# A decode step (cached attention plus GeGLU gate): the last wo rows cut by partitions, x in two loads, wo's first quarter ahead of w_down, 14 drains on SP

## The chip, the core and the metric

The kernel runs on one core of a Trainium2 chip, as one launch. The metric is device time in microseconds (us); of several executions the median is taken. Lower is better.

## The reference, cut to what matters

One token for each of 8 sequences goes through a layernorm, then through two branches that both read the normed row: attention over the last 1024 positions of a cache (32 query heads, 8 key/value heads of 128), projected by wo, and a gated feed-forward net. The second branch gates the first.

```python
xn = layernorm(x)                                   # x: 8 x 512, bf16
q  = xn @ wq                                        # wq: 512 x 4096
p  = softmax(q @ k[last 1024].T * 128**-0.5)        # k, v: 8 x 8 x 4096 x 128; 16 MB each are read
s  = (p @ v[last 1024]) @ wo                        # wo: 4096 x 512
f  = (gelu(xn @ w_gate) * (xn @ w_up)) @ w_down     # 512 x 1792 twice, 1792 x 512
out = x + s * silu(f)
```

## The kernel before, in words

Everything is in one function, and its order is written out by hand: each engine runs its instructions in the order of the source.

**Loads.** Nearly all loads are issued from SP's queue, in this order: wo's first quarter (`wo_first`, L106), wq (L109), then K and V of the eight sequences, each as two transfers of 1 MB (`load_cache`, L84), then w_gate and w_up (L426), w_down (L429), and wo's other three quarters (L439). The last quarter of wo comes in three pieces along its 8 rows per partition: rows 0 to 4, 5 to 6, and row 7 alone (1 KB in each of 128 partitions). x (8 rows of 1 KB) comes in four loads of two rows from ACT's queue (L79). The tile framework gives every DMA one of eight completion semaphores in turn. A DMA waits on its issuing queue until the one that had its semaphore before has landed, so at most eight are under way. K and V go through a ring of eight buffers; two of these use wq's memory once q is computed.

**Attention.** For each sequence: DVE turns K (`turn_k`, L248), PE makes the scores (L309), DVE and ACT do the softmax, PE makes the values (L354), and `gather` (L374) and `regroup` (L376 to L398) put the outputs of four sequences at a time into `oT`, the stationary operand of the wo product.

**The end.** After the last `regroup`, PE runs in this order: z and u (xn by w_gate and w_up, L453), then f (the hidden row by w_down, L482, 28 matmuls), then s (`oT` by wo, L501, 64 matmuls: quarters u = 0 to 3, rows j = 0 to 7, two halves each). Between u and f stands a chain on ACT and DVE, the gelu (L463 to L473), that ends in the transpose `hT` (L476). The last product is gated and added to x (L509, L511), and two DMAs write the output (L514). The quarter u = 0 reads `wo_first`, which was loaded at the very start.

```python
for u in range(NU):                      # L498
    for j in range(8):
        for t in range(NT):
            nc.tensor.matmul(s_ps[32*t : 32*t + 32, :], oT[:, j, u, :],
                             wo[u][:, j, t*DT : (t+1)*DT], ...)
```

Of the kernel before, what the change touches and what calls it, by code (L numbers as in the profile page):

```python
# [11 lines left out]
FP32 = mybir.dt.float32  # L12
# [8 lines left out]
def kernel(  # L21
# [13 lines left out]
    nc = tc.nc  # L35
# [9 lines left out]
    P = nc.NUM_PARTITIONS  # L45
# [7 lines left out]
    NT = 2  # L53
    DT = D // NT
# [12 lines left out]
    def slot(name):  # L67
        i = taken[0] % N_SLOTS
        taken[0] += 1
        if i >= 2:  # L70
            return ring.tile([P, 2 * ROW], BF16, name=name, tag="slot")
        if not late:
            late.append(ctx.enter_context(tc.tile_pool(name="late", bufs=2)))
        return late[0].tile([P, 2 * ROW], BF16, name=name, tag="slot")


    x_sb = keep.tile([B, D], BF16, name="x_sb")
    for r, z in ((0, 2), (2, 4), (4, 6), (6, 8)):
        nc.scalar.dma_start(out=x_sb[r:z], in_=A_x.flatten_outer_dims()[r:z])  # L79

    def load_cache(cache, b, name):
        t = slot(name).rearrange("p (g x) -> p g x", g=NG)
        for g in range(NG):
            nc.sync.dma_start(  # L84
                out=t[:, g],
                in_=cache[b, g * HG : (g + 1) * HG, win0:Sk, :].rearrange(
                    "n (p c) d -> p n (c d)", c=C
                ),
            )
        return t  # L90
# [3 lines left out]
    def load_k(b):  # L94
        k_sb[b] = load_cache(A_k_cache, b, "k_sb")

    def load_v(b):
        v_sb[b] = load_cache(A_v_cache, b, "v_sb")

    NU = Hq // 8  # L100
    wo_src = [
        A_wo[u * 1024 : (u + 1) * 1024, :].rearrange("(p j) d -> p j d", j=8)
        for u in range(NU)
    ]
# [6 lines left out]
    load_k(0)  # L111
    load_k(1)
    load_v(0)


    ident = consts.tile([P, P], BF16, name="ident")
# [2 lines left out]
        out=ident,  # L119
        in_=ident,  # L120
# [13 lines left out]
        out=xpad,  # L134
        in_=xpad,
# [17 lines left out]
        out=xhat,  # L153
# [8 lines left out]
    with tc.tile_pool(name="ps_x", bufs=1, space=PSUM) as ps_x:  # L162
# [7 lines left out]
        for t in range(NT):  # L170
# [4 lines left out]
                start=True,  # L175
                stop=True,
# [12 lines left out]
        out=hv,  # L189
        in_=hv,  # L190
# [7 lines left out]
        out=neg_st,  # L198
        in_=neg_st,
# [8 lines left out]
        out=neg_mv,  # L208
        in_=neg_mv,
# [11 lines left out]
    for g in range(NG):  # L221
        nc.vector.tensor_reduce(
            out=sel[:, g, g * qd : (g + 1) * qd],
            in_=ident.rearrange("p (t g h) -> p g h t", t=4, g=NG)[:, g],
# [5 lines left out]
        out=own, in_=ident.rearrange("p (i e) -> p e i", e=8), axis=AX.X, op=ALU.add  # L230
    )
    pick = consts.tile([P, 4 * NU], BF16, name="pick")
    with nc.allow_low_precision(reason="sums of zeros and a single one"):
        nc.vector.tensor_reduce(
            out=pick, in_=ident.rearrange("p (a e) -> p a e", e=8), axis=AX.X, op=ALU.add
        )
    oT = keep.tile([P, 8, NU, 32], BF16, name="oT")
# [18 lines left out]
    with tc.tile_pool(name="ps_q", bufs=1, space=PSUM) as ps_q:  # L256
        q_ps = [ps_q.tile([P, 512], FP32, name=f"q_ps{i}") for i in range(8)]
        for k in range(NK):
            for i in range(8):
# [4 lines left out]
                    start=(k == 0),  # L264
                    stop=(k == NK - 1),
                )
        for half in range(2):
            for i in range(4 * half, 4 * half + 4):
                e = nc.vector.tensor_copy if i % 4 == 3 else nc.scalar.copy
# [7 lines left out]
    for j in range(4):  # L277
        sl = slice(32 * j, 32 * j + 32)
        for m in range(2):
            for g in range(NG):  # L280
                e = nc.scalar.copy if (4 * j + 2 * m + g) % 3 == 2 else nc.vector.tensor_copy
# [148 lines left out]
    wo = [wo_first]  # L430
    for u in range(1, NU):
        if u % 2 == 1:
            pair = slot("wo_sb").rearrange("p (v j d) -> p v j d", v=2, d=D)
        t = pair[:, (u - 1) % 2]
        pieces = [(0, 8)]
        if u == NU - 1:
            pieces = [(0, 5), (5, 7), (7, 8)]
        for a, z in pieces:
            nc.sync.dma_start(out=t[:, a:z, :], in_=wo_src[u][:, a:z, :])  # L439
        wo.append(t)  # L440

    gather(B - 1)
# [3 lines left out]
    ps_f = ctx.enter_context(tc.tile_pool(name="ps_f", bufs=1, space=PSUM))  # L446
    ffn = ctx.enter_context(tc.tile_pool(name="ffn", bufs=1))
    zu = []
    for n, ws in (("z_ps", wgu[0]), ("u_ps", wgu[1])):
        ps = ps_f.tile([P, FT], FP32, name=n)  # L450
        for k in range(NK):
            for t in range(4):
# [4 lines left out]
                    start=(k == 0),  # L457
                    stop=(k == NK - 1),
# [6 lines left out]
        out=z2, in0=z2, scalar1=0.044715, scalar2=1.0, op0=ALU.mult, op1=ALU.add  # L465
# [10 lines left out]
    nc.vector.transpose(  # L476
        out=hT.rearrange("p j b -> p (j b)"), in_=h_bf.rearrange("p (y j) -> p j y", j=NJ)
    )
    f_ps = ps_f.tile([32 * NT, DT], FP32, name="f_ps")
    for j in range(NJ):  # L480
        for t in range(NT):
# [4 lines left out]
                start=(j == 0),  # L486
                stop=(j == NJ - 1),
# [4 lines left out]
        out=g_sb, in0=g_sb, scalar1=0.5, scalar2=0.5, op0=ALU.mult, op1=ALU.add  # L492
# [1 line left out]
    nc.vector.tensor_tensor(out=g_sb, in0=g_sb, in1=f_ps, op=ALU.mult)  # L494


    s_ps = ps_f.tile([32 * NT, DT], FP32, name="s_ps")
    for u in range(NU):  # L498
        for j in range(8):
            for t in range(NT):  # L500
                nc.tensor.matmul(  # L501
                    s_ps[32 * t : 32 * t + 32, :],
                    oT[:, j, u, :],
                    wo[u][:, j, t * DT : (t + 1) * DT],
                    start=(u == 0 and j == 0),
                    stop=(u == NU - 1 and j == 7),
                )
    y = ffn.tile([32 * NT, DT], BF16, name="y")
    nc.vector.tensor_tensor(out=y, in0=s_ps, in1=g_sb, op=ALU.mult)  # L509
    out_sb = ffn.tile([32 * NT, DT], BF16, name="out_sb")  # L510
# [2 lines left out]
    for t, e in ((0, nc.sync), (1, nc.scalar)):  # L513
        e.dma_start(  # L514
            out=out_f[:, t * DT : (t + 1) * DT], in_=out_sb[32 * t : 32 * t + B, :]
# [31 lines left out]
```

## Time and profile before

| | |
|---|---|
| median of 3 runs | 120.83 us (120.79 to 120.89) |
| the profiled execution's own time | 120.78 us |
| its span, first to last instruction | 118.9 us |
| busy: PE / DVE / ACT / POOL | 62% / 64% / 28% / 3% of the span |
| DMA | 47.57 MB, mean 400 GB/s; SP's queue took 95.0% of 16 engines' span |
| K and V loads, issue to landing | 19.6 us for 1 MB |

The profile's page cuts the span into 40 equal slices of 2.97 us. A digit is a busy share in tenths; PEclk is the clock that the throttle granted to TensorE. The chain of waits is followed back from the last instruction, at each step to what released it. Idle time of an engine that is not on that chain costs nothing by itself. A table by windows gives busy time of each engine, the granted clock and the mean busy share of the 16 DMA engines for stretches of the span.

### The profile page before, as it was taken

The page shows a single profiled execution, that of the slowest core. Times are in us where ns is not written, and L with a number is a line of the kernel's source. Part 1 is how long each engine was busy: PE and PEld are TensorE (multiplying, and loading weights), DVE is VectorE, ACT ScalarE, POOL GpSimd, SP SyncE. Part 2 cuts the span into 40 slices and gives each one's busy share as a digit, 9 for nine tenths or more (in the row PEclk, how much of TensorE's full clock was granted, in tenths as well). Part 3 has the DMA queues.
Part 4 walks back from the last instruction along what each step waited for, and adds up shares of the span by engine and source line. Part 5 has one row for each costly group of instructions (what it writes and reads, how often), then busy time and mean ns, then how long its engine had stood idle before and what let it go on. Part 6 is the DMA issues. An engine that isn't in the chain of part 4 may idle for free.

```text
span 118.9 us, 1553 instructions
## 1 busy us (share of the span) xinstructions
PE 74.1 (62%) x610; PEld 35.2 (30%) x610; DVE 75.8 (64%) x101; ACT 33.1 (28%) x83; POOL 3.2 (3%) x10
## 2 busy tenths in 40 slices
PE   0000279941599596969964867598299263854990
PEld 0000123410233253435432324134035131413780
DVE  1002779389998999999956995980994224165102
ACT  2100600096202518171531341071070811110100
POOL 2000430000000000000000000000000000000000
PEclk9999999999679999999999999679859955555599
DMA  3999899999999999999999999999999999999940
GB/s 59 472 453 431 353 433 427 419 438 427 427 424 427 430 424 422 427 419 435 427 408 435 433 422 430 433 422 424 424 430 419 459 415 444 405 426 430 412 153 3
DMA packets 6103, 47.57 MB, mean 400 GB/s; under 512 B 696, under 2 KB 848, under 8 KB 1104
## 3 DMA queue, kind: packets, MB, share of 16 engines
q1 hardware_dynamic: 6064, 47.45, 95.0%
q8 instruction: 5, 0.08, 0.2%
q10 hardware_dynamic: 32, 0.01, 0.0%
q14 instruction: 2, 0.02, 0.0%
HBM read 47.46 MB, written 0.01 MB: 399 GB/s over the span
## 4 chain that ended last, share of the span: by engine, by line
DMA 60%; PE 24%; DVE 9%; ACT 3%; issue 1%; SPq 0%; DVEq 0%
DMA k_sb<-in_A_k_cache_dram 49%; DMA wq_sb<-in_A_wq_dram 12%; PE q_ps L260 8%; PE S_ps L309 5%; PE s_ps L501 3%; PE f_ps L482 3%; DVE kT L248 2%; PE O_ps L354 2%; PE z_ps L453 1%; PE o_ps L374 1%; ACT P_sb L332 1%; DVE o_x L381 1%; DVE mx L319 1%; DVE hT L476 1%; ACT nb L329 1%
## 5 line engine op out<-in xcount | busy, mean ns | idle before, releaser
L309 PE MATMUL S_ps<-kT,qbd 128*128 128x512 bf16 x128 | 35.0, 421 | 16.2 <-DVE kT L248 12.8
L248 DVE STREAM_TRANSPOSE kT<-k_sb 128x2048 int32<-128x2048 int32 x16 | 36.5, 2289 | 5.2 <-DMA k_sb<-in_A_k_cache_dram 5.2
L309 PEld LDWEIGHTS <-qbd 128*128 128x128 bf16 x128 | 13.0, 103 | 35.4 <-issue 20.3
L329 ACT ACTIVATE nb<-m 32x1 f32<-32x1 f32 x32 | 6.4, 201 | 23.5 <-DVE m L326 23.2
L332 ACT ACTIVATE P_sb<-S_ps,nb 128x1024 bf16<-128x1024 f32 x8 | 11.1, 1391 | 0.3
L354 PE MATMUL O_ps<-v_sb,pT 128*32 128x256 bf16 x256 | 9.3, 292 | 2.7 <-DVE pT L344 2.7
L260 PE MATMUL q_ps<-wq_sb,xnR 128*128 128x512 bf16 x32 | 9.5, 469 | 2.4 <-DMA wq_sb<-in_A_wq_dram 2.4
L319 DVE TENSOR_REDUCE mx<-S_ps 128x1 f32<-128x1024 f32 x8 | 9.6, 1195 | 1.8 <-PE S_ps L309 1.8
L366 ACT COPY O_sb<-O_ps 128x256 f32<-128x256 f32 x8 | 3.0, 374 | 21.6 <-PE O_ps L354 21.6
L354 PEld LDWEIGHTS <-pT 128*32 128x32 bf16 x256 | 6.5, 102 | 6.3 <-issue 3.0
L166 PE MATMUL xnT_ps<-ident,xhat 8*128 8x8 bf16 x4 | 0.3, 174 | 12.6 <-DVE xhat L152 12.6
L344 DVE STREAM_TRANSPOSE pT<-P_sb 128x512 int32<-128x512 int32 x8 | 5.7, 712 | 3.4 <-ACT P_sb L332 3.0
L145 DVE BATCH_NORM_STATS2 stats<-x_sb 8x6 f32<-8x512 bf16 x1 | 0.7, 681 | 9.4 <-DMA x_sb<-in_A_x_dram 9.4
L374 PE MATMUL o_ps<-O_sb,sel 128*32 128x129 f32 x32 | 5.5, 297 | 1.0 <-ACT O_sb L366 1.0
L260 PEld LDWEIGHTS <-xnR 128*128 128x128 bf16 x32 | 3.6, 115 | 8.0 <-issue 5.9
L298 PE MATMUL S_ps<-neg_mv,neg_st 128*128 128x512 bf16 x16 | 4.8, 382 | 1.9 <-DVE q_both L270 1.9
L270 ACT CAST q_both<-q_ps 128x512 bf16<-128x512 f32 x6 | 3.0, 611 | 10.0 <-PE q_ps L260 10.0
L482 PE MATMUL f_ps<-wd_sb,hT 128*32 128x256 bf16 x28 | 3.2, 419 | 3.1 <-DVE hT L476 3.1
L374 PEld LDWEIGHTS o_ps<-O_sb,sel 128*32 128x32 f32 x32 | 3.1, 116 | 4.9 <-issue 3.1
L251 DVE MEMSET qbd<- 128x4096 uint32 x1 | 3.5, 3472 | 0.8 <-issue 0.8
L166 PEld LDWEIGHTS <-xhat 8*128 8x128 bf16 x4 | 0.2, 114 | 12.6 <-DVE xhat L152 12.6
L501 PEld LDWEIGHTS <-oT 128*32 128x32 bf16 x64 | 3.6, 107 | 0.7
(64 smaller groups left out, 51.1 us busy)
## 6 DMA issues: line engine op xcount, KB each, us to landing
k_sb<-in_A_k_cache_dram SPq DMA_DIRECT2D x16, 1024.0 KB, 19.6
v_sb<-in_A_v_cache_dram SPq DMA_DIRECT2D x16, 1024.0 KB, 19.6
wq_sb<-in_A_wq_dram SPq DMA_DIRECT2D x1, 4096.0 KB, 14.2
wo_sb<-in_A_wo_dram SPq DMA_DIRECT2D x2, 1024.0 KB, 25.0
wgu_sb<-in_B_w_gate_dram SPq DMA_DIRECT2D x1, 1792.0 KB
wgu_sb<-in_B_w_up_dram SPq DMA_DIRECT2D x1, 1792.0 KB
wd_sb<-in_B_w_down_dram SPq DMA_DIRECT2D x1, 1792.0 KB
wo_first<-in_A_wo_dram SPq DMA_DIRECT2D x1, 1024.0 KB, 4.9
```

The costliest lines, as they stand in the source:

```text
L248: nc.vector.transpose(out=t.bitcast(I32), in_=k_sb[b][:, g].bitcast(I32))
L260: nc.tensor.matmul(q_ps[i], xnR[:, k, :, :].rearrange("p j b -> p (j b)"), wq_sb[k][:, i * 512 : (i + 1) * 512], start=(k == 0), stop=(k = ...
L298: nc.tensor.matmul(S[b][:, half, :], neg_st.rearrange("p j h -> p (j h)"), neg_mv.rearrange("p a n -> p (a n)"), start=True, stop=False,)
L309: nc.tensor.matmul(S[b][:, half, :], qbd[:, m, b, w, g, :], kv[:, half * 16 : (half + 1) * 16, m, :, w], start=False, stop=(g == NG - 1 an ...
L319: nc.vector.tensor_reduce(out=mx, in_=S[b].rearrange("p a c -> p (a c)"), axis=AX.X, op=ALU.max)
L329: nc.scalar.mul(nb[32 * j : 32 * j + 32, :], m1, -inv)
L332: nc.scalar.activation(out=P_sb[b].rearrange("p c i w -> p c w i"), in_=S[b].rearrange("p a (c w i) -> p (a c) w i", w=2, i=32), func=ACT.Exp,
L344: nc.vector.transpose(out=pT[b].rearrange("p c h w -> p (c h w)").bitcast(I32), in_=P_sb[b].rearrange("p c i w -> p (c i w)").bitcast(I32),)
L354: nc.tensor.matmul(O_ps[b][32 * t : 32 * t + 32, :, :], pT[b][:, c // 2, :, c % 2], vv[:, c, :, :], start=(c < 4), stop=(c >= C - 4),)
L374: nc.tensor.matmul(o, sel[:, g, :], O_sb[b][:, g, :], start=(g == 0), stop=(g == NG - 1))
L482: nc.tensor.matmul(f_ps[32 * t : 32 * t + 32, :], hT[:, j, :], wd[:, j, t * DT : (t + 1) * DT], start=(j == 0), stop=(j == NJ - 1),)
L501: nc.tensor.matmul(s_ps[32 * t : 32 * t + 32, :], oT[:, j, u, :], wo[u][:, j, t * DT : (t + 1) * DT], start=(u == 0 and j == 0), stop=(u = ...
```

## The change

- The last quarter's row 7 (`(7, 8)`, 1 KB in each of 128 partitions) is no longer one transfer: partitions 0 to 31, 32 to 116 and 117 to 127 are loaded by a transfer each (32, 85 and 11 partitions), from the same queue.
- x comes in two loads of four rows, not four of two.
- The s product of quarter u = 0 (16 matmuls) stands before the f product, in PE's order; quarters 1 to 3 stay behind it. The tile `s_ps` is allocated earlier.
- 14 drain instructions stand on SP's queue behind the first three K/V loads. With the two added transfers, SP's program goes from 76 to 92 instructions.

```diff
-    for r, z in ((0, 2), (2, 4), (4, 6), (6, 8)):
+    for r, z in ((0, 4), (4, 8)):
         nc.scalar.dma_start(out=x_sb[r:z], in_=A_x.flatten_outer_dims()[r:z])
...
     load_k(0)
     load_k(1)
     load_v(0)
+    for _ in range(14):
+        nc.sync.drain()
...
-        pieces = [(0, 8)]
+        pieces = [(0, 8, 0, P)]
         if u == NU - 1:
-            pieces = [(0, 5), (5, 7), (7, 8)]
-        for a, z in pieces:
-            nc.sync.dma_start(out=t[:, a:z, :], in_=wo_src[u][:, a:z, :])
+            pieces = [(0, 5, 0, P), (5, 7, 0, P), (7, 8, 0, 32), (7, 8, 32, 117), (7, 8, 117, P)]
+        for a, z, r, e in pieces:
+            nc.sync.dma_start(out=t[r:e, a:z, :], in_=wo_src[u][r:e, a:z, :])
...
+    s_ps = ps_f.tile([32 * NT, DT], FP32, name="s_ps")
+
+    def project(u):
+        for j in range(8):
+            for t in range(NT):
+                nc.tensor.matmul(
+                    s_ps[32 * t : 32 * t + 32, :],
+                    oT[:, j, u, :],
+                    wo[u][:, j, t * DT : (t + 1) * DT],
+                    start=(u == 0 and j == 0),
+                    stop=(u == NU - 1 and j == 7),
+                )
+
+    project(0)
     f_ps = ps_f.tile([32 * NT, DT], FP32, name="f_ps")
...
-    s_ps = ps_f.tile([32 * NT, DT], FP32, name="s_ps")
-    for u in range(NU):
...
+    for u in range(1, NU):
+        project(u)
```

More of the change, by code (lines that the diff above doesn't have):

```diff
@@ L494 @@
     nc.vector.tensor_tensor(out=g_sb, in0=g_sb, in1=f_ps, op=ALU.mult)
-    s_ps = ps_f.tile([32 * NT, DT], FP32, name="s_ps")
-    for u in range(NU):
[L499 to L507, printed above, removed]
+    for u in range(1, NU):
+        project(u)
     y = ffn.tile([32 * NT, DT], BF16, name="y")
```

## The prediction

> **What bounds the kernel now.** I read the page first, then the windows and the chain of waits at the end, then the waits of PE and SP. In the 40 slices (part 2 of the page):
>
> ```profile
> PEclk9999999999679999999999999679859955555599
> DMA  3999899999999999999999999999999999999940
> GB/s 59 472 453 431 353 433 427 419 438 427 427 424 427 430 424 422 427 419 435 427 408 435 433 422 430 433 422 424 424 430 419 459 415 444 405 426 430 412 153 3
> ```
>
> The DMA engines are full from the second slice to slice 38, at about 427 GB/s, and TensorE's clock is at half from about 95 us until shortly before the end. So the stream of bytes sets nearly everything, and what remains is how the last bytes and the last matmuls meet. The chain of waits over the last 11 us, in order of time (start, length, what):
>
> ```profile
> 107.65 0.99 DVE hT L476
> 108.64 0.04 issue
> 108.69 3.17 PE f_ps L482 x28
> 111.86 4.00 PE s_ps L501 x60
> 115.86 0.02 issue
> 115.88 0.43 DVE y L509
> ```
>
> By this the end is compute: f, then s without a gap. The windows (length, busy time of PE, PEld, DVE, ACT, POOL, granted clock, DMA share, GB/s) show the transfers beside it:
>
> ```profile
> 105.89:109.31 3.42, 0.62 (x8) 0.45 (x10) 2.57 (x4) 0.00 (x0) 0.00 (x0) 0.50 0.96 408
> 109.31:112.72 3.41, 3.41 (x36) 2.49 (x34) 0.31 (x2) 0.38 (x1) 0.00 (x0) 0.50 0.99 416
> 112.72:114.10 1.38, 1.38 (x28) 1.25 (x26) 0.39 (x1) 0.00 (x0) 0.00 (x0) 1.00 0.83 320
> 114.10:115.50 1.40, 1.40 (x30) 1.26 (x27) 0.00 (x0) 0.00 (x0) 0.00 (x0) 1.00 0.25 87
> ```
>
> The last row matters most: for 1.4 us only a quarter of the DMA engines still works. The trace's completion events of the last transfer (row 7 of wo's last quarter) say the same: ten of its 16 parts end at 113.93 to 114.15 us, two at 114.65 and 114.77, four at 115.34 to 115.50. The piece before it (rows 5 and 6) ends at 115.165, rows 0 to 4 at 114.566, wo's third quarter at 113.022. The last pair of matmuls starts at 115.561. So PE is on the chain, but the last bytes stand only 0.06 us behind it: two bounds that coincide.
>
> Why six engines are late can be read too. The page's DMA queues show instruction loads:
>
> ```profile
> q8 instruction: 5, 0.08, 0.2%
> q14 instruction: 2, 0.02, 0.0%
> ```
>
> By the start of their packets they come at 33.6 and 57.4 us (8 KB) and 44.5, 59.1, 84.2, 99.8 and 114.8 us (16 KB). Behind each of the first six, one more engine's completions fall back, by 0.7 to 0.9 us for 8 KB and 1.3 to 1.8 us for 16 KB, and stay behind to the end, since SP's queue is never empty. Two light and four heavy ones are the two and four above.
>
> **The change part by part.** The sum is made against the profiled execution, 120.78 us (span 118.9 us and 1.9 around it), 0.05 under the median.
>
> *Quarter 0 before f.* It takes 16 matmuls from between f and quarter 1. They start at 111.65 and quarter 1 at 113.05: 1.40 us off PE's last stretch. They go where PE waits:
>
> ```profile
> PE f_ps L482 <- DVE hT L476: 3.1, 1, 3.1
> ```
>
> u ends at 105.58 and f may start at 108.69. At the half clock a pair takes 0.209 us (f's rows), so 8 pairs take 1.67: 105.4 to 107.2. `oT` was ready at 102.17, wo_first at 5.7. Cover left: 1.4 us, so no cost. If the cover were gone, f would wait up to 1.67 us. The clock rose at 112.72, after a window that PE had filled; f and quarter 1 fill the same window. The window before it becomes about 0.5 busy, where ones of 0.72 and 0.78 raised nothing. So f stays at half clock until 111.65, then quarter 1: five pairs at 0.209 to 112.72, three at 0.108, to 113.03. Quarter 2 finds its bytes (113.022) and runs to 113.93. Then PE waits, for the first time in this stretch. From completion to the matmul it released took 0.043 us (w_up at 103.843, u at 103.886). Row 0 of quarter 3 starts at 114.61, row 5 at 115.165 + 0.043 = 115.21, row 6 at 115.32, row 7 at 115.425 or at its own landing plus 0.043, the later. With the old row 7 transfer that is 115.544: 0.017 us gained of 1.40. What is late next is the transfer.
>
> *Row 7 in three.* In this trace the engines of one transfer always take equal shares: x's 2-row load completes in two steps, the 8-row output in eight, 128 rows in 16 of 8 rows each. So 32 rows go as 2 to each of 16. 85 is 5 times 17, so equal shares mean 5 engines with 17 rows or one with 85; 11 rows mean 11 with one. The price of a row: between rows 5 to 6 and row 7 the slowest engine spent 0.336 us on 8 rows, 0.042 each. An engine outside the five carries 2 or 3 rows, not 8, and lands 0.21 to 0.25 us sooner; one of the five carries 19 or 20, 0.46 to 0.50 later. If the four heavy engines are outside, row 7 lands at 115.25 to 115.31 with a completion packet or two more (0.01 each), under the 115.38 at which row 6 gives way; the ten on time reach 114.6, a light one 115.27. The bounds are far apart: the 85 rows on all 16 engines give nothing (115.50), on one engine alone 85 x 0.042 = 3.6 us, so 117.5 from an engine on time. I take five, since one is the extreme and no transfer here is uneven. Whether the four are outside the five is the open question. I followed packets by their start times from the two engines that carried x's rows: neither met a 16 KB load before 114 us, one perhaps the 8 KB load at 57.4 (engines in the same phase can't be told apart, so this is weak). If x's two are of the five, four heavy ones miss the other three with about 0.33 if strewn at random over 14, about 0.7 if they are neighbours. I take 0.6, the likelier side.
>
> The Trainium skill ("DMA: Bandwidth & Descriptors", Why a DMA increments its semaphore by 16 and not by 1) says that a transfer uses the largest number up to 16 that divides its slowest dimension, on the lowest-numbered engines: 16, 5 and 11 here. The trace agrees for 2, 8 and 128 rows; no run here shows 85. The Trainium skill's same page (Rules for kernel authors) speaks against the change: cutting a transfer by partitions isn't worth it, and under 64 KB one pays mostly overhead. By its table's figure for 64 KB, 0.95 us (measured on loads issued from GpSimd), an estimate for three in a row would be 2.85 us, 2.5 more than now; the trace's last piece, 128 KB queued behind another, cost 0.34 us, so it disagrees, and this gets no chance of its own.
>
> *x in two loads.* Two loads less on ACT, 0.24 us each, beside nothing. SP's waits name x:
>
> ```profile
> SPq L84 <- DMA x_sb<-in_A_x_dram: 3.2, 2, 1.9
> SPq L84 <- DMA wq_sb<-in_A_wq_dram: 4.3, 1, 4.3
> ```
>
> x's later rows land behind big packets of the other queue (5.7, 8.1, 10.6 us), so two loads land by about 5.7, and the layernorm moves up 5 us. It still ends at wq, landed at 15.47. SP may issue two K/V loads sooner, into a queue that is full anyway. Zero, hidden by wq; at most the 0.1 us of a few packets either way.
>
> *14 drains.* SP's drains last 7 to 13 ns and its instructions stand 0.06 us apart, so 0.2 to 0.9 us on SP, with the next K load behind them. It finds 9 us of wq ahead of it in the queue: hidden; without that cover, 0.9. But a longer program can load one block more: ACT (97 recorded instructions) and DVE (117) each did, SP (72) did not, and it will have 88. By where 88 lies between 72 and 97, I give that 0.6. It costs one engine 0.7 us, nothing unless it is one of the four late ones (1 in 4).
>
> Sum: row 7's pair at 115.425 instead of 115.561, 0.14 less; 120.64 for the profile, 120.69 for the median. That is within 0.2% (0.24 us), about what a measurement of this kernel can tell from no change. Terms unsure by 0.05 each and the completion delays put it between 120.45 and 120.9.
>
> **The rivals.**
> - *A heavy engine is among the five* (slower). Place: row 7's 85-row transfer; price: 12 rows more on a late engine, 0.50, so 116.00 + 0.043 instead of 115.561. 121.31, with 121.2 to 121.4 around it. It decides as soon as one of the four takes part. For: five of 16 is much. Against: x's engines looked clean. Chance 0.23.
> - *SP's own load falls on a late engine*: 0.7 us behind the rest at the end, 115.30 + 0.7 + 0.043 against 115.561, so 121.3. Chance 0.6 x 0.25, less what counts above: 0.08.
> - *The longer program moves the loads to better places.* If no heavy engine is late at the end but the light ones (114.77) are, row 7's pair starts near 114.85 to 115.0, and 0.55 to 0.7 us go: 120.2. For: lateness is all that holds the end above 114.1, and 14 drains touch only program layout. Against: five loads follow TensorE's count, which does not change. Chance 0.20.
> - *The split does nothing* (85 rows on all engines): only 0.02 of the move is left, 120.81. Chance 0.04.
>
> **How the numbers follow.** Forecast 0.45: a third of it (0.15) lies beyond 0.24 us, 0.01 above. Faster 0.15 + 0.20 = 0.35; same 0.29 + 0.04 = 0.33; slower 0.01 + 0.23 + 0.08 = 0.32. The range, 120.2 to 121.4, takes in both sides and leaves out about 0.15. The forecast's own is 120.45 to 120.9.
>
> **What would show it.** 16 s matmuls between 105.4 and 107.2 us; a wait of PE for wo_sb of about 0.7 us before row 0 of quarter 3; row 7's last completion at 115.25 to 115.31; PE's last pair at 115.42; no new stretch of idle DMA before 113 us. Wrong: row 7 landing near 116.0 (the five hold a late engine); a third 8 KB load and a fifth late engine; a different count of late engines at the end; f starting later than 108.7.

## The result, and the profile after

The changed kernel takes 120.95 us (median of 21 executions, 120.77 to 121.45), against 120.79 us (120.50 to 121.16) for 21 executions of the kernel before on the same chip. The ratio is 1.0021, 95% interval 1.0013 to 1.0029. The forecast was 0.14 us less; measured is 0.16 us more by the medians, 0.25 by the ratio.

The profiled execution is one of the changed kernel's fastest: 120.80 us, span 119.1 (the median span is 119.2) and 1.7 around it (before: 118.9 and 1.9). The page's clock and DMA slices, its instruction loads and its chain:

```profile
PEclk9999999999589999999999999999769955577699
DMA  2998899999999999999999999999999999999930
q8 instruction: 5, 0.08, 0.3%
q14 instruction: 4, 0.02, 0.1%
DMA 95%; PE 1%; DVE 1%; issue 0%; SPq 0%
```

The stream is as full as before. There are two more instruction loads on q14: 8 KB at 118.47 us, and 80 bytes at the span's start. The chain that ended last is now DMA to 95%; before, its end was PE. The same chain piece by piece (start, length, what):

```profile
90.28 24.36 DMA wo_sb<-in_A_wo_dram
114.64 0.04 issue
114.68 1.29 PE s_ps L486 x16
115.98 0.02 issue
116.00 0.43 DVE y L516
```

f and 44 of the 60 s matmuls have left it: the end now hangs on wo's last quarter. The gated product `y` starts at 116.00, against 115.88 before. The timeline of the last 12 us shows how PE got there (start, length, line, operation, idle before and its releaser in brackets):

```profile
105.11 1.22 PE L486 MATMUL s_ps<-wo_first,oT 128*32 128x256 bf16 x16
...
108.40 2.77 PE L498 MATMUL f_ps<-wd_sb,hT 128*32 128x256 bf16 x28 [2.07 <-DVE hT L478]
...
110.96 1.69 PE L486 MATMUL s_ps<-wo_sb,oT 128*32 128x256 bf16 x16
...
112.82 1.05 PE L486 MATMUL s_ps<-wo_sb,oT 128*32 128x256 bf16 x16 [0.17 <-DMA wo_sb<-in_A_wo_dram]
...
114.68 1.28 PE L486 MATMUL s_ps<-wo_sb,oT 128*32 128x256 bf16 x16 [0.82 <-DMA wo_sb<-in_A_wo_dram]
```

Quarter 0 runs in the wait for `hT`, which still leaves 2.07 us of it. Quarters 2 and 3 now wait for their bytes, 0.17 and 0.82 us. Quarter 3 then takes 1.28 us, where 1.05 is a quarter without a wait at full clock: its last pair starts at 115.677, after row 7. The windows (length, busy time of PE, PEld, DVE, ACT, POOL, granted clock, DMA share, GB/s):

```profile
105.45:108.86 3.41, 1.34 (x26) 1.02 (x24) 2.61 (x4) 0.08 (x1) 0.00 (x0) 1.00 0.96 407
108.86:112.28 3.42, 3.42 (x38) 2.53 (x34) 0.56 (x2) 0.38 (x1) 0.00 (x0) 0.50 1.00 422
112.28:114.10 1.82, 1.42 (x22) 1.04 (x19) 0.14 (x1) 0.00 (x0) 0.00 (x0) 1.00 0.87 333
114.10:115.70 1.60, 1.02 (x16) 0.69 (x15) 0.00 (x0) 0.00 (x0) 0.00 (x0) 1.00 0.18 60
```

The last row is the place of the change. Before, a quarter of the DMA engines still worked for the last 1.4 us; now 0.18 of them, for 1.6 us. Row 7's bytes did end sooner: the last completion packet runs at 114.971 us, before at 115.214. But the completions come later behind their packets. In us, by the trace's DMA packets and completion events:

```
                                          before    after   forecast
wo rows 0 to 4, last completion          114.566  114.640  114.566
wo rows 5 and 6, last completion         115.165  115.272  115.165
row 7: last completion packet            115.214  114.971
row 7: last completion                   115.501  115.541  115.25 to 115.31
  of it 32 / 85 / 11 partitions             -     115.422 / 115.359 / 115.541
from that packet to that completion        0.287    0.570
last pair of s matmuls starts            115.561  115.677  115.425
output, last landing                     118.095  118.178
from that landing to the span's end        0.830    0.908
```

The last two lines count too. From the last pair to the output's landing it is 2.53 us before and 2.50 after; behind the landing SP still has its last waits to work through, and there the change loses another 0.08 us.

### The profile page after: what moved, and what is told of

Read it like the earlier page. It is cut to its first block, busy times and chain, and to the rows that moved or that the text cites. A ratio compares the mean times of both kernels' runs of the same rounds, so it can differ in the third digit from the quotient of the medians.

```text
span 119.1 us, 1559 instructions
## 1 busy us (share of the span) xinstructions
PE 71.7 (60%) x603; PEld 35.3 (30%) x610; DVE 76.0 (64%) x101; ACT 33.1 (28%) x83; POOL 3.2 (3%) x10
## 4 chain that ended last, share of the span: by engine, by line
DMA 95%; PE 1%; DVE 1%; issue 0%; SPq 0%
DMA v_sb<-in_A_v_cache_dram 71%; DMA wo_sb<-in_A_wo_dram 20%; DMA wo_first<-in_A_wo_dram 4%; PE s_ps L486 1%; DVE y L516 0%; DVE out_sb L518 0%; SPq L441 0%
## 5 line engine op out<-in xcount | busy, mean ns | idle before, releaser
L311 PE MATMUL S_ps<-kT,qbd 128*128 128x512 bf16 x128 | 33.2, 406 | 18.6 <-DVE kT L250 15.1
L486 PE MATMUL s_ps<-wo_sb,oT 128*32 128x256 bf16 x48 | 4.0, 310 | 1.0 <-DMA wo_sb<-in_A_wo_dram 1.0
L300 PE MATMUL S_ps<-neg_mv,neg_st 128*128 128x512 bf16 x9 | 3.3, 384 | 1.9 <-DVE q_both L272 1.9
L272 DVE CAST q_both<-q_ps 128x512 bf16<-128x512 f32 x2 | 1.3, 672 | 3.9 <-ACT q_both L272 3.9
```

Source lines behind the costliest of these rows:

```text
L272: e(out=q_bf[:, i * 512 : (i + 1) * 512], in_=q_ps[i])
L311: nc.tensor.matmul(S[b][:, half, :], qbd[:, m, b, w, g, :], kv[:, half * 16 : (half + 1) * 16, m, :, w], start=False, stop=(g == NG - 1 an ...
L486: nc.tensor.matmul(s_ps[32 * t : 32 * t + 32, :], oT[:, j, u, :], wo[u][:, j, t * DT : (t + 1) * DT], start=(u == 0 and j == 0), stop=(u = ...
```

## The experiments

The theories that the expectations name. **P**: transfers over part of the partitions make the engines' completions late. **W**: each further small transfer costs by itself, whatever its form. **F**: PE's last 16 KB instruction load, which moved up to 113.9 us, slows the late engines. **D**: the drains decide which engines are late. B, C, X and N are explained where they first stand; C of e7 and e8 is another theory than C of e12. The table puts all runs together, each against the kernel before on the same chip. Its last two columns are of the one profiled execution: the start of the last pair of s matmuls (of e9's second matmul), and the time from the output's last landing to the span's end.

| kernel | SP's instructions | median us | ratio to before | median span | time less span | last pair | landing to end |
|---|---|---|---|---|---|---|---|
| before (beside each) | 76 | 120.67 to 120.79 | | 118.8 to 118.9 | 1.86 to 1.89 | 115.561 | 0.830 |
| the change | 92 | 120.95 | 1.0021 [1.0013, 1.0029] | 119.2 | 1.73 | 115.677 | 0.908 |
| e1: the move alone | 76 | 120.72 | 1.0002 [0.9989, 1.0016] | 118.85 | 1.87 | 115.738, half clock | 0.823 |
| e2: the split alone | 78 | 121.22 | 1.0044 [1.0028, 1.0059] | 119.3 | 2.02 | 115.882 | 0.987 |
| e3: the change, row 7 whole | 90 | 121.16 | 1.0042 [1.0030, 1.0054] | 119.5 | 1.74 | 115.995, half clock | 1.393 |
| e4: the change, no drains | 78 | 121.37 | 1.0055 [1.0040, 1.0070] | 119.25 | 2.11 | 115.691 | 0.883 |
| e5: x in two alone | 76 | 120.85 | 1.0018 [1.0004, 1.0031] | 119.0 | 1.87 | 115.775 | 0.944 |
| e6: 16 drains alone | 92 | 120.61 | 0.9991 [0.9982, 0.9999] | 118.9 | 1.71 | 115.449 | 0.835 |
| e7: row 7 as 48, 48, 32; 14 drains | 92 | 121.64 | 1.0080 [1.0060, 1.0099] | 119.9 | 1.73 | 116.081 | 1.348 |
| e8: row 7 as 125, 3; 15 drains | 92 | 120.73 | 0.9999 [0.9988, 1.0010] | 119.0 | 1.77 | 115.463 | 0.839 |
| e9: row 7 in column halves; 15 drains | 92 | 120.84 | 1.0014 [1.0002, 1.0026] | 119.1 | 1.73 | 115.587 | 1.040 |
| e10: row 7 in partition halves; 15 drains | 92 | 121.03 | 1.0028 [1.0017, 1.0040] | 119.3 | 1.73 | 115.749 | 1.044 |
| e11: 2 drains alone | 78 | 121.00 | 1.0017 [1.0006, 1.0028] | 118.9 | 2.09 | 115.310 | 0.823 |
| e12: the move, PE kept busy, 16 drains | 92 | 120.59 | 0.9987 [0.9978, 0.9996] | 118.8 | 1.75 | 115.466 | 0.835 |

The last column is no constant, and several verdicts below turn on it. SP ends the program with six waits in a fixed order, 0.06 to 0.09 us apart where nothing holds them, that take in all eight DMA semaphores. In the kernel before, the output's two transfers have the semaphores of the last two waits. The DMAs take the eight semaphores in turn, so a load more or less gives the output other ones, and then further waits follow its last landing: one in the change and e4, two in e3 and e5, three in e2, e7, e9 and e10. (In e8 the order is e9's, but there the part of the output that stands in the last wait lands last.) From the last pair to the landing it is 2.50 to 2.55 us in every profiled execution, 2.71 at the half clock.

**e1, the move alone.**

```diff
+    project(0)
     f_ps = ps_f.tile([32 * NT, DT], FP32, name="f_ps")
...
-    for u in range(NU):
+    for u in range(1, NU):
+        project(u)
```

> The kernel before with quarter 0 of the s product ahead of f, and nothing else. Theory W (the three transfers of row 7 pay a fixed price each and three waits on PE): without them rows 5 and 6 land near 115.17, row 7 near 115.50, the last pair starts near 115.54; 0.0 to 0.1 us faster than before. Theory F (TensorE's fifth 16 KB instruction load, which comes at 113.9 instead of 114.8 us once PE reaches quarter 3 earlier, slows the late engines): the load starts near 113.9, packets of 2 KB take up to 130 ns instead of 84 near it, rows 5 and 6 land near 115.27, row 7 near 115.6, the last pair near 115.65; 0.1 us slower than before.

No change: at the median the move gains nothing, as the prediction had it. The profiled execution (121.12 us) shows what the move can bring with it. Its windows and its timeline:

```profile
110.99:114.41 3.42, 1.52 (x26) 1.13 (x23) 0.00 (x0) 0.00 (x0) 0.00 (x0) 1.00 0.86 345
114.41:115.90 1.49, 1.49 (x16) 1.15 (x15) 0.00 (x0) 0.00 (x0) 0.00 (x0) 0.50 0.08 29
```

```profile
112.79 1.05 PE L484 MATMUL s_ps<-wo_sb,oT 128*32 128x256 bf16 x16 [1.40 <-DMA wo_sb<-in_A_wo_dram]
114.34 1.86 PE L484 MATMUL s_ps<-wo_sb,oT 128*32 128x256 bf16 x16 [0.49 <-DMA wo_sb<-in_A_wo_dram]
```

PE is ahead of its bytes, waits 1.40 and 0.49 us, and in the window after that its clock is at half: quarter 3 takes 1.86 us, and its last pair starts 0.5 us behind row 7, which had landed at 115.246. The granted clock changes on a grid of 3.41 us in every trace here; the grid's place differs from one execution to the next. The Trainium skill says the same ("TensorE: Matmul & The Clock Gate", What's actually happening): a free-running window of 3.4 us.

The other side of it is seen in the kernel before, where the clock may come late. Of 79 executions of it with a listed clock, 23 had a mean clock under 0.878, and in each of three batches these took 0.2 to 0.4 us more than the rest; of 58 executions of the five kernels with the move, one had.

**e12, the move with PE kept busy.** 16 matmuls whose sums nobody reads stand before quarter 3, and 16 drains on SP.

```diff
+        if u == NU - 1:
+            for j in range(8):
+                for t in range(NT):
+                    nc.tensor.matmul(warm_ps[32 * t : 32 * t + 32, :], oT[:, j, 0, :],
+                                     wo[0][:, j, t * DT : (t + 1) * DT], ...)
         project(u)
```

> The kernel before with quarter 0 ahead of f, 16 drains (92 instructions on SP) and 16 matmuls more, whose sums nobody reads, ahead of quarter 3 where PE waits for rows 0 to 4. Theory C (quarter 0 ahead of f makes PE idle near the end, so that in some executions the clock falls to half and the last eight pairs take 0.21 us each instead of 0.11): with PE kept busy the clock stays up, the last pair follows the last completion by 0.05 us, the span is 118.7 to 118.8 in nearly all executions and the time about 120.5, the fastest so far. Rival (the move does nothing in any case): 120.6, as with 16 drains alone.

In the windows of its profile the clock stays up to the end:

```profile
111.04:114.45 3.41, 1.94 (x37) 1.74 (x34) 0.00 (x0) 0.00 (x0) 0.00 (x0) 1.00 0.83 332
114.45:115.70 1.25, 1.25 (x24) 1.06 (x20) 0.00 (x0) 0.00 (x0) 0.00 (x0) 1.00 0.15 49
```

By the ratios (0.9987; e6, on another chip, 0.9991) it stands within 0.05 us of e6: beside the drains, which both have, the move gains nothing clear of noise even with PE kept busy, since the last pair (115.466) stands 0.1 us behind row 7's landing (115.371). With the 0.043 us from landing to matmul, at most 0.05 of that is due to the added matmuls.

**e2, the split alone.**

```diff
-            pieces = [(0, 5), (5, 7), (7, 8)]
+            pieces = [(0, 5, 0, P), (5, 7, 0, P), (7, 8, 0, 32), (7, 8, 32, 117), (7, 8, 117, P)]
```

> The kernel before with row 7 in three transfers of 32, 85 and 11 partitions, and nothing else (x in four loads, no drains, so two DMAs more). Theory W: rows 5 and 6 land near 115.17, the three transfers add 0.27 us on the late engines, row 7 is complete near 115.43, the last pair waits for three semaphores in a row and starts near 115.57 to 115.6: the same as before within 0.05 us. Theory F: the instruction load comes at 114.8, rows 0 to 6 land as before. Theory D (the drains decide which engines are late): the 85-row transfer now has a heavy engine among its five, one of its five completions comes near 116.0 and the kernel is 0.4 us slower.

Slower by 0.5 us: 0.44 in the span of the profiled executions, the rest around it. Of the 0.44, 0.32 stand at the last pair and 0.16 behind the output's landing. Row 7's last completion came 0.84 us behind its last packet (before: 0.29). The 85-row transfer's five completions come at 114.57 to 115.20, no heavily late engine among them.

**e3 and e4, the change without one of its parts.** e3 loads row 7 in one transfer; e4 has no drains.

```diff
-            pieces = [(0, 5, 0, P), (5, 7, 0, P), (7, 8, 0, 32), (7, 8, 32, 117), (7, 8, 117, P)]
+            pieces = [(0, 5, 0, P), (5, 7, 0, P), (7, 8, 0, P)]        # e3
-    for _ in range(14):                                               # e4
-        nc.sync.drain()
```

> The changed kernel with row 7 in one transfer of 128 partitions (90 instructions on SP). Theory W: one transfer of 0.34 us on the late engines instead of two of 0.27 in all, but one wait instead of three: the last pair starts 0.0 to 0.05 us earlier or later than in the changed kernel; the time is between before and after. Theory F: rows 5 and 6 still land near 115.27, row 7 near 115.6, the last pair near 115.65, as slow as the changed kernel.

> The changed kernel without the 14 drains (78 instructions on SP). Theories W and F: the same time as the changed kernel within 0.1 us, the same four heavy and two light late engines, row 7 complete near 115.54. Theory D: another set of engines is late; one of the five completions of the 85-row transfer comes near 116.0, and the kernel is 0.3 to 0.5 us slower than with the drains.

Both are slower than the full change, against what W said. Both also change the length of SP's program, to 90 and 78. In e4 the five completions of the 85 partitions come at 114.46 to 115.27, much as in the change, so D falls, though its 0.3 to 0.5 us came true as a number; e4 loses 0.4 us to the change, nearly all of it outside the span. In e3 the span holds a stall of SP: between two of its waits at the end, 0.07 us apart elsewhere, it stands for 0.47 us, 118.722 to 119.195, right behind the output's landing at 118.706, and an 8 KB instruction load follows at 119.83. Before has neither. In the change the same stall lies at 117.158 to 117.640, and the output lands at 118.18: it is hidden. In all seven kernels with 92 instructions the stall follows the second of the six waits, in e3, with two instructions less, the fourth; and e3's output, with two loads less, has the semaphores of the third and fourth waits, right ahead of it. The waits of SP in the last 10 us (waited for, in total, times, longest) show it in e6, whose stall lies there too, and in before, which has none:

```profile
SPq L544 <- DMA out_dram<-out_sb: 0.2, 1, 0.2
```

```profile
SPq L542 <- DMA out_dram<-out_sb: 0.6, 1, 0.6
```

In e6, the first, 0.4 us of the wait for the output have gone under the stall. (e3's profiled execution also had the half clock of e1 in its last quarter: last pair 115.995, row 7 landed 115.518.)

**e6 and e11, SP's length alone.** Nothing else is changed: 16 drains, or two, behind `load_v(0)`.

```diff
+    for _ in range(16):   # e6; e11: range(2)
+        nc.sync.drain()
```

> The kernel before with 16 drains on SP, so 92 instructions there, and nothing else. Theory B: SP crosses into a further block of its program while the output is under way; the span stays at 118.8, what lies around it falls from 1.89 to about 1.73 us, and the kernel is 0.15 us faster than before. Rival (drains only cost): the time is as before or up to 0.3 us slower.

> The kernel before with 2 drains on SP (78 instructions), and nothing else. Theory B (the block of SP's program): the block is loaded behind the span's end, the span stays at 118.8, what lies around it grows from 1.87 to about 2.1 us, and the kernel is 0.2 us slower than before, 0.35 us slower than with 92. Rival (the program's length doesn't matter): as before.

The spans are equal (118.9; before: 118.8 and 118.9), the times are not: less the span, 1.71 us with 92 instructions, 1.87 with 76, 2.09 with 78. SP's load follows: at 118.12 us in e6, at 120.61 in e11, behind the span's end, and none in before. So two instructions more cost 0.2 us and sixteen more save 0.15: the place of a block's border in SP's last instructions decides, as the stall that moves by two waits with two instructions says too. The split's two transfers take 76 to 78, and the drains bring that to 92; between the change and e4 they are worth 0.38 around the span. The Trainium skill ("Runtime: NRT & Kernel Launch", Instruction fetch mechanics) has fetches in blocks of 256 instructions and 16 KB, mostly hidden. The runs agree with blocks; these loads of SP are 8 KB, and the stall ahead of one is the 0.4 us above where nothing hides it.

**e5, x in two loads alone.**

```diff
-    for r, z in ((0, 2), (2, 4), (4, 6), (6, 8)):
+    for r, z in ((0, 4), (4, 8)):
```

> The kernel before with x in two loads, and nothing else (76 instructions on SP). Theory W (transfer price and waits) and theory B (the block of SP's program that is loaded at the end) both say: no change, within 0.05 us, span 118.8. Rival X (two loads less shift the eight semaphores, and with them what each load waits for): the span grows by about 0.2 us, which would be the part of the kernel with row 7 whole (span 119.5) that the 0.4 us stall of SP leaves unexplained.

It costs about 0.15 us, all in the span. It is no matter of the clock's place alone: the seven executions with a mean clock over 0.878 stand at 120.8, 24 of before on that chip at 120.65. In the profile 0.11 us of it lies behind the output's landing (0.944 against 0.830): with two loads less the output has the semaphores of the third and fourth waits, and two waits of 0.06 us follow. So the semaphores do shift, as rival X said, but the loss that the trace shows is in SP's last waits, not in the loads. The change has as many loads as the kernel before, so this loss is not in it.

**e7 and e8, other splits by partitions.**

```diff
+            pieces = [..., (7, 8, 0, 48), (7, 8, 48, 96), (7, 8, 96, P)]   # e7
+            pieces = [..., (7, 8, 0, 125), (7, 8, 125, P)]                 # e8
```

> The kernel before with row 7 in three transfers of 48, 48 and 32 partitions (3, 3 and 2 rows on every engine) and 14 drains (92 instructions on SP). Theory W: 0.09 us a transfer and engine and 0.03 a row, so row 7 takes 0.51 us on the late engines instead of 0.34, and three waits in a row add 0.09: span about 119.05, no packets of 2 KB over 90 ns, 0.25 us slower than the kernel with 92 instructions and one transfer. Theory C (85 rows on five engines slow the late engines' packets): with even shares rows 5 and 6 land as before, and the loss is smaller than with 32, 85 and 11.

> The kernel before with row 7 in two transfers of 125 and 3 partitions (25 rows on each of five engines, then one on each of three) and 15 drains (92 instructions on SP). Theory W alone: the heavy engines carry nothing of row 7 and end with rows 5 and 6, near 115.17; the light ones among the five end near 115.35; two waits; the last pair stays where PE can have it, 115.56, span 118.8, as fast as the kernel with 92 instructions and one transfer. Theory C: packets of 2 KB take up to 130 ns while the five engines work, rows 5 and 6 land near 115.35, the span is 118.9 to 119.1.

e7, three transfers on all 16 engines, is the slowest: each transfer's last completion stands 0.20 us behind the one before (rows 5 and 6 at 115.342, then 115.546, 115.749, 115.946). Only about half of its loss to e6 is row 7's, however: its last pair starts 0.63 us later, and 0.51 us more lie behind the output's landing (1.348 against 0.835), since the output's waits stand right at SP's stall. e8's 125 partitions end in five completions, the 3 in three; it equals before, but with the drains' 0.15 in its favour; against e6 it loses 0.12. C of these two texts is not borne out: in e7 rows 5 and 6 land late all the same, in e8 the packets of 2 KB take at most 91 ns and rows 5 and 6 land at 115.205.

**e9 and e10, two transfers in both ways.** Both halve row 7 and have SP at 92. e9 halves its 512 columns, all 128 partitions in each; e10 its partitions, whole rows in each.

```diff
+            nc.sync.dma_start(out=t[:, a:z, r:e], in_=wo_src[u][:, a:z, r:e])
+            pieces = [..., (7, 8, 0, 256), (7, 8, 256, D)]   # e9: columns r to e
+            pieces = [..., (7, 8, 0, 64), (7, 8, 64, P)]     # e10: partitions r to e
```

> The kernel before with row 7 in two transfers of 128 partitions and half the columns each (512 B), and 15 drains (92 instructions on SP). Theory P (a transfer over part of the partitions lets engines write into each other's part of SBUF, and completions come late): every engine keeps its own 8 partitions, so the time from completion packet to landing stays at 0.30 to 0.36 us, row 7 lands at most 0.1 us later than with one transfer, the span is 118.8 to 118.9. Rival N (it is the number of transfers and completions that counts): the delay grows to 0.45 us or more, as with 64 partitions twice, and the span is 119.1 or more.

> The kernel before with row 7 in two transfers of 64 partitions (4 rows of 1 KB on every engine in each) and 15 drains (92 instructions on SP): as many transfers, completions and waits as with the two column halves. Theory P: the time from completion packet to landing grows from 0.33 to 0.5 us or more while they run, row 7 lands 0.2 to 0.4 us later, the span is 119.1 to 119.3. Rival N: the same as with column halves, within 0.1 us.

This is the pair that tells P from W. With the same number of transfers and completions, the last completion comes 0.296 us behind its packet in e9 (before: 0.287) and 0.471 in e10, up to 0.65 on other engines; e10's row 7 lands at 115.706, e9's at 115.545, and the medians differ by 0.19 us, with the same time behind the landing (1.04). So P holds in what it says of the completions: they are late with part of the partitions, not by the number alone. That engines write into each other's part of SBUF is not shown. The other profiled executions agree: with row 7 whole or cut by columns, rows 5 and 6 land at 114.912 to 115.187; with row 7 cut by partitions, at 115.205 to 115.389.

W's price for a further transfer is smaller than e9's time suggests. e9 loses 0.23 us to e6 (measured on another chip), but in the profiles 0.21 lie behind the output's landing (1.040 against 0.835), where the one load more has put three waits. At the landing itself, row 7 ends 0.378 us behind rows 5 and 6 in e9, and 0.318 to 0.336 behind them in the seven executions with row 7 whole: about 0.05 us for the further transfer. The Trainium skill ("DMA: Bandwidth & Descriptors", Rules for kernel authors), which the prediction had set aside, holds in its direction: halving by partitions costs, e10 against e6 0.42 us, of which 0.21 lie behind the output's landing.

F falls: in e1 and e3 PE's load comes at 113.83 and 114.06 and no late engine's packets are slower; in the change they are (2 KB in up to 133 ns instead of 84), and in e2 too, up to 144, though PE's load comes only at 114.94 there.

## Why the prediction was wrong

**Right.** The bound: the last bytes, not PE. The move: 16 matmuls between u and f, hidden, f no later (108.40), a wait of 0.82 us before quarter 3 (0.7 forecast), and no gain at the median. Its clock came otherwise: it was full from 105.45 to 108.86, where half was forecast, so that quarter 2 waited for its bytes as well; that cost nothing, since the bytes set the end. The five engines: the 85-partition transfer ended in exactly five completions (114.668, 114.688, 114.785, 115.145, 115.359), the 11-partition one in eleven. No heavily late engine was among the five, so the likeliest placement came true, and with again two light and four heavy late engines the rivals of placement fell. The bytes ended 0.24 us sooner, as 0.21 to 0.25 had said; part of that is the execution, since in the seven with row 7 whole the last packet runs anywhere from 114.944 to 115.237. The further block of SP's program was loaded, but at 118.47 us, when no transfer of the stream was left to delay.

**The step that failed: "row 7 in three".** The term "with a completion packet or two more (0.01 each)" priced the two further transfers at 0.02 us. The landing was 115.541 instead of 115.31, 0.57 us behind its packet. Followed to the last pair: rows 5 and 6 landed 0.107 late, which alone moves row 7's pair from 115.425 to 115.53; row 7's landing plus 0.043 makes it 115.584; and it started at 115.677, since three transfers are three semaphores, and PE took their waits one behind the other: 0.136 us from the last landing to the matmul, not 0.043 (0.135 in e2, e4 and e7, which have three as well). So all of the 0.24 us that the engines gained was lost again between packet and landing, and the waits came on top. The landings do not overlap: 115.246 to 115.518 in the seven executions with row 7 whole, 115.541 to 115.747 in the three cut as 32, 85 and 11. e10 beside e9 shows that it is the cut by partitions that makes completions late; the further transfer by itself is some 0.05 us (e9), not 0.01.

**Two terms set at zero.** The drains were priced by what they do to SP's queue ("0.2 to 0.9 us on SP ... hidden") and its further block by the engine that fetches it. What they did lies around the span, which the sum carried over as 1.9: it is 1.73 in the change. That is a gain of 0.15 us, and 0.38 against the change without drains. "x in two loads", at "zero", cost 0.15 by e5, most of it in SP's last waits; in the change the two further loads put the output back on its old semaphores. One wait still follows its landing there, the 0.08 us above.

**The sum as measured**, between the two profiled executions (120.78 and 120.80 us): the last pair starts 0.116 us later, from there to the output's landing it is 0.033 shorter, from the landing to the span's end 0.078 longer, and around the span 0.141 shorter, 0.02 in all. The forecast had the pair 0.136 earlier and the rest unchanged, so the pair alone was off by 0.25 us. The medians differ by 0.16 us, since the changed kernel's profiled execution is among its fastest; where its other executions lose the rest is in no trace here. That the forecast was missed by no more than 0.26 us is in part luck: the drains gave 0.14 that it did not have.

**Open.** Why completions of part of the partitions come late: the Trainium skill ("SBUF — State Buffer", Door 1: The DMA port swizzle) has partitions 0 to 63 reach only half the ports, which would fit e10 beside e9, but no run here separates ports from other causes. Other counts of drains than 2, 14 to 16 and none were not tried, nor e9's columns with the move.

Two kernels beat both: e6, which is the kernel before with 16 drains (0.9991, interval 0.9982 to 0.9999), and e12 (0.9987, 0.9978 to 0.9996). The gain is SP's, about 0.15 us around the span.

## What to carry to other kernels

When the last piece of a stream sets the end, count three times for it, not one: its last packet, its completion, and the waits of the consumer; a cut that frees the packets sooner can lose more in the other two. Look behind the output's landing before a loss is put down to a transfer: a load more, or two less, gave the output another semaphore here, and SP's last waits then took up to 0.2 us more without any stall. Look at the time around the span too: instructions that cost nothing on their queue can move an instruction load at the program's end into or out of sight. And a move that makes an engine wait shortly before the end can bring its clock down for the end itself.

## What the runs showed of the hardware

- From the last completion packet to the last completion it is 0.28 to 0.35 us in the kernels whose late transfers cover all 128 partitions (also in e9 with one transfer more), and 0.35 to 0.84 in those cut by partitions.
- 85, 11, 125, 3 and 64 partitions end in 5, 11, 5, 3 and 16 completions.
- Where an instruction load of SP's follows inside the span, SP stands for 0.47 us ahead of it, about 0.4 of it added time where nothing hides it; 78 instructions against 76 cost 0.2 us, 92 save 0.15.
- Three semaphores ahead of one matmul took 0.136 us from the last landing, one took 0.043.
- From the output's landing to the span's end it is 0.82 to 0.84 us where its semaphore stands in SP's last wait, 1.04 where three waits follow, 1.35 to 1.39 where SP's stall follows as well.
- The 3.41 us grid on which the granted clock changes lies elsewhere in each execution. In e1's and e3's profiled ones PE had half the clock in its last quarter, which took 1.86 and 1.82 us instead of 1.05.
